# The first load of a soft-MoE kernel: one transfer of 128 rows, or four of 32 rows with a step of four partitions

## Chip, cores and metric

The kernel runs on one core of a Trainium2 chip. The metric is the device time in microseconds, the median over runs. Three runs of the kernel before took 174.36, 174.44 and 174.56 us. One more execution was profiled; its trace gives the rows below.

## What is computed

Linear attention over 8 batches of 8 heads, followed by a soft mixture of 8 experts with 4 slots each:

```python
# q, k, v: (8, 8, 576, 64)
kv  = einsum('bhsd,bhse->bhde', k, v)
out = einsum('bhsd,bhde->bhse', q, kv)
out = out / sqrt(mean(out*out, -1) + 1e-6) * g_norm
x   = out as (4608, 512)                     # tokens x (heads*dim)
logits = x @ phi                             # phi: (512, 32)
d = softmax of logits over the tokens
slot_input = d.T @ x                         # (32, 512), 4 slots for each expert
slot_out[e] = relu(slot_input[e] @ w1[e]) @ w2[e]   # w1: 512 x 1024, w2: 1024 x 512
c = softmax of logits over the slots
return c @ slot_out                          # (4608, 512)
```

All data is float32.

## The kernel before

The inputs are laid out on the host so that each load is one transfer of 128 rows, one row for each partition of SBUF. Nearly everything lands in one tile, `arena`, whose places are used again as data is done with. All loads and stores are issued by SP, in the order of the program, on one queue.

The first load, `first_in`, is 128 rows of 2448 floats: the router weights phi and g_norm (the first 144 columns), and the first half of k and v of batch 0. Behind it SP issues the second half of batch 0 (`kv_in`), half of q of the first pair of batches (`q0_in`), the two halves of kv of batch 1, the rest of `q0_in`, kv of batch 2 and part of `q1_in`. Line numbers: the first load is L123, and the others go through `load_row` (L85). The later ones wait until PE is done with the place that they fill.

PE begins with matmuls on constants (L457 and L467, `fill`), which need no load. Then, for each batch, it forms the 64 x 64 products of k and v from the loaded rows, contracting over 128 partitions (`Kv.products`, L195, and the border rows, L210), transposes them and multiplies them with phi (L224, L226). ACT and DVE copy the result into the block-diagonal tiles `bd`, and PE multiplies q with these, token tile by token tile (`products`, L263). DVE scales phi by g_norm once (`gphi`, L158), out of the first load. The statistics of the softmax over the tokens are kept as the tiles go by. After the last tile come the experts (`expert_h`, L638, and `expert_y`, L656, with the weights loaded by `load_w`, L114) and the outputs (L701, stored at L718).

The completion of a load is signalled by one of eight semaphores, `DMAHW0` to `DMAHW7`, which the framework hands out in turn, in the order of the issues. The ninth load takes the first one's semaphore again, and its issue waits until that earlier load has landed.

Of the kernel before, what the change touches and what calls it, by code (L numbers as in the profile page):

```python
# [55 lines left out]
HEAD = 144  # L56
# [10 lines left out]
def soft_moe_linear_attention(ctx: ExitStack, tc: tile.TileContext, first_in, kv_in, q0_in, q1_in, kv4_in, kv5_in, t3_in, w_in, out):  # L67


    nc = tc.nc  # L70
# [3 lines left out]
    arena = const.tile([P, HEAD + ARENA], F32, name="arena")  # L74
# [9 lines left out]
    def load_row(at, src):  # L84
        nc.sync.dma_start(place(at, src.shape[-1]), src)  # L85
# [34 lines left out]
        return parts[k][:, at : at + 256]  # L120


    nc.sync.dma_start(arena[:, : HEAD + 2304], first_in)  # L123
    load_row(KV_AT[0] + 9, kv_in[0, :, 2304:])
    load_row(Q_AT[0], q0_in[:, :2048])
    load_row(KV_AT[1], kv_in[1, :, :2304])
# [297 lines left out]
    first = {b: 9 * (b // 2) + 4 * (b % 2) for b in range(B)}  # L424
# [341 lines left out]
def build_program():  # L766
    import concourse.bacc as bacc

    nc = bacc.Bacc("TRN2", target_bir_lowering=False, num_devices=1, dynamic_dma_scratch_size=SCRATCH)
    shapes = {  # L770
        "first": (P, HEAD + 2304), "kv": (4, P, TOK), "q0": (P, TOK), "q1": (P, 2048),
        "kv4": (P, 2560 + TOK), "kv5": (P, 2 * TOK), "t3": (P, 3 * TOK),
        "w": (1, 2 * NE * P * UNIT),
    }
    args = [nc.dram_tensor(f"in_{n}_dram", s, F32, kind="ExternalInput").ap() for n, s in shapes.items()]
    args.append(nc.dram_tensor("out_0_dram", (1, 4 * NCH * P * 4 * CT * NS), F32, kind="ExternalOutput").ap())
    with tile.TileContext(nc, schedule_with_timeline_sim=True) as tc, tc.manual_schedule():
        soft_moe_linear_attention(tc, *args)
    return nc
# [58 lines left out]
```

## Time and profile before

| what | value |
|---|---|
| median of 3 runs | 174.44 us (174.36 to 174.56) |
| span of the profiled execution | 172.9 us |
| PE busy | 150.1 us (87%) |
| DVE, ACT, POOL busy | 86.3, 89.0, 57.2 us |
| moved by DMA | 71.67 MB, mean 414 GB/s |
| busy share of the 16 DMA engines, the program's own queue | 97.0% |
| mean granted clock of TensorE | 0.976 |

The span runs from the first to the last instruction of the profiled execution. The profile gives no other time for that execution; the median of the runs, which take in what lies around the span, is 1.5 us longer. "Idle" in a row of an engine is the time just before the instruction in which the engine did nothing, and behind the arrow stands what ended it. Windows of DMA count a packet, with all its bytes, where it starts.

### The profile page before, as it was taken

To read this page: it belongs to the slowest core of one execution; us is meant where nothing else is said; L and a number is where in the kernel's file an instruction comes from. 1 tells how busy PE (TensorE), PEld (TensorE's weight loads), DVE (VectorE), ACT (ScalarE), POOL (GpSimd) and SP (SyncE) were. 2 spreads that over 40 slices of the span, in tenths; PEclk is the share of its full clock that TensorE was granted. 3 is DMA by queue.
4 is the path that set the end of the run, shared out by engine and by line. 5 is a ranking of instruction groups with operands and counts; after the bars stand their busy time and mean duration, and the time that the engine had idled before them with its cause. 6 is when DMAs were issued, how large, how long until landed. Compare 5 with 4: busy or idle time off the path is not lost.

```text
span 172.9 us, 4638 instructions
## 1 busy us (share of the span) xinstructions
PE 150.1 (87%) x1975; PEld 109.0 (63%) x1975; DVE 86.3 (50%) x184; ACT 89.0 (51%) x230; POOL 57.2 (33%) x68
## 2 busy tenths in 40 slices
PE   7888897989999899999899989889999989989300
PEld 3457777889688888898796766346665544545000
DVE  1122156383677364763926897625887036228300
ACT  2036486787966888668759863203223035227400
POOL 6000708548356665456582489100000000000000
PEclk9999999999999999999999999999999999999955
DMA  5999999999999998999999998999999999999994
GB/s 188 417 429 426 446 403 449 438 424 471 413 409 443 479 461 359 394 453 402 451 468 428 426 425 368 426 445 400 459 419 428 425 425 403 443 392 401 453 392 199
DMA packets 3476, 71.67 MB, mean 414 GB/s; under 512 B 384, under 2 KB 384, under 8 KB 384
## 3 DMA queue, kind: packets, MB, share of 16 engines
q1 hardware_dynamic: 3456, 71.38, 97.0%
q8 instruction: 15, 0.25, 0.6%
q14 instruction: 5, 0.04, 0.1%
HBM read 61.94 MB, written 9.44 MB: 413 GB/s over the span
## 4 chain that ended last, share of the span: by engine, by line
PE 50%; DMA 23%; ACT 10%; DVE 6%; issue 3%; SPq 2%; DVEq 0%
PE o L263 16%; DMA arena<-in_kv_dram 13%; DMA arena<-in_w_dram 10%; PE kvp_kv L195 8%; PE po L701 5%; PE pY L656 5%; PE pS L412 4%; PE ph L638 2%; PE fill L467 2%; ACT sq L273 2%; PE o L254 2%; ACT arena L712 2%; ACT bd L230 1%; ACT xall L281 1%; SPq L85 1%
## 5 line engine op out<-in xcount | busy, mean ns | idle before, releaser
L263 PE MATMUL o<-bd,arena 128*128 128x192 f32 x256 | 49.3, 336 | 1.7 <-ACT bd L240 1.1
L263 PEld LDWEIGHTS o<-bd,arena 128*128 128x128 f32 x256 | 40.8, 190 | 5.0 <-ACT bd L240 1.6
L286 DVE TENSOR_REDUCE ms<-sq 128x16 f32<-128x1024 f32 (+1 forms) x19 | 22.1, 1162 | 32.2 <-ACT sq L273 32.0
L313 POOL TENSOR_TENSOR xall<-xall,r 128x512 f32<-128x512 f32 x34 | 34.8, 1046 | 0.0
L335 POOL TENSOR_TENSOR part<-part,r 128x512 f32<-128x512 f32 x17 | 17.8, 1050 | 50.4 <-DVE r L304 44.9
L273 ACT ACTIVATE sq<-o 128x512 f32<-128x512 f32 x36 | 21.5, 598 | 11.9 <-PE o L263 11.6
L281 ACT COPY xall<-o 128x512 f32<-128x512 f32 x34 | 20.6, 606 | 0.0
L195 PE MATMUL kvp_kv<-arena 128*64 128x64 f32 x480 | 17.3, 225 | 2.6 <-DMA arena<-in_kv_dram 1.9
L195 PEld LDWEIGHTS kvp_kv<-arena 128*64 128x64 f32 x480 | 15.2, 138 | 6.5 <-DMA arena<-in_kv_dram 2.8
L348 DVE TENSOR_REDUCE logits<-part 128x64 f32<-128x512 f32 (+1 forms) x18 | 17.8, 992 | 0.0
L656 PE MATMUL pY<-arena,xall 128*32 128x256 f32 x256 | 15.0, 380 | 0.2 <-DMA arena<-in_w_dram 0.2
L701 PE MATMUL po<-logits,z 32*128 32x384 f32 x96 | 12.8, 521 | 1.5 <-ACT arena L712 0.9
L638 PE MATMUL ph<-arena,sTe 128*32 128x256 f32 x224 | 12.7, 379 | 0.3 <-DVE sTe L585 0.3
L712 ACT COPY arena<-po 128x768 f32<-128x768 f32 x12 | 9.1, 801 | 7.4 <-PE po L701 7.4
L714 DVE COPY arena<-po 128x768 f32<-128x768 f32 x10 | 9.3, 955 | 7.0 <-PE po L701 7.0
L656 PEld LDWEIGHTS pY<-arena,xall 128*32 128x32 f32 x256 | 8.4, 110 | 6.7 <-issue 1.6
L280 ACT COPY part<-o 128x256 f32<-128x256 f32 x34 | 12.6, 370 | 0.0
L412 PE MATMUL pS<-xall,d 128*32 128x129 f32 x288 | 10.8, 277 | 1.2 <-ACT d L400 1.1
L701 PEld LDWEIGHTS po<-logits,z 32*128 32x128 f32 x96 | 6.1, 183 | 7.1 <-ACT arena L712 4.2
L638 PEld LDWEIGHTS ph<-arena,sTe 128*32 128x32 f32 x224 | 7.2, 110 | 5.3 <-DVE sTe L585 0.7
L412 PEld LDWEIGHTS pS<-xall,d 128*32 128x32 f32 x288 | 7.2, 109 | 4.4 <-issue 3.5
L294 ACT ACTIVATE r<-ms,eps 128x16 f32<-128x16 f32 x17 | 5.2, 308 | 5.9 <-DVE ms L286 5.9
(99 smaller groups left out, 148.3 us busy)
## 6 DMA issues: line engine op xcount, KB each, us to landing
arena<-in_w_dram SPq DMA_DIRECT2D x4, 4096.0 KB, 19.8
arena<-in_w_dram SPq DMA_DIRECT2D x1, 7168.0 KB, 27.6
arena<-in_t_dram SPq DMA_DIRECT2D x1, 6912.0 KB, 36.4
arena<-in_w_dram SPq DMA_DIRECT2D x1, 5120.0 KB, 17.8
arena<-in_kv_dram SPq DMA_DIRECT2D x2, 2304.0 KB, 23.6
arena<-in_kv_dram SPq DMA_DIRECT2D x1, 4608.0 KB, 43.1
out_dram<-arena SPq DMA_DIRECT2D x2, 2304.0 KB, 9.5
arena<-in_kv_dram SPq DMA_DIRECT2D x1, 3584.0 KB, 32.3
```

The costliest lines, as they stand in the source:

```text
L195: nc.tensor.matmul(self.pkv[lo : lo + 64, w, g], lhsT=main[:, w, 1, c, lo : lo + 64], rhs=main[:, w, 0, c, lo : lo + 64], start=c == 0 and ...
L263: nc.tensor.matmul(o[:, r, :192], lhsT=q_main(2 * g + i)[:, r, at : at + P], rhs=bds[i][:, r], start=True, stop=True)
L273: nc.scalar.activation(sqs[s][:, T - starts[s]], o[:, :, 32:160], AF.Square, scale=0.125)
L281: nc.scalar.copy(xts[T % NX][:, :, :128], o[:, :, 32:160])
L286: nc.vector.tensor_reduce(out=mss[s], in_=sqs.pop(s).rearrange("p t j (w d) -> p (t j w) d", w=2), axis=AX.X, op=ALU.add)
L313: nc.gpsimd.tensor_tensor(out=x, in0=x, in1=r[:, i].rearrange("p (j w) -> p j w", w=2).unsqueeze(3).to_broadcast([P, 4, 2, D]), op=ALU.mult,)
L335: engine.tensor_tensor(out=part, in0=part, in1=rs_of[s].unsqueeze(3).to_broadcast([P, STAGES[s], H, NS]), op=ALU.mult)
L348: nc.vector.tensor_reduce(out=L[:, pos(starts[s]) : pos(starts[s]) + STAGES[s]], in_=parts.pop(s).rearrange("p t h n -> p t n h"), axis=AX ...
L412: nc.tensor.matmul(pS[32 * j : 32 * j + 32], lhsT=ds[G][:, i], rhs=x[:, j], start=i == 0, stop=i == GROUPS[G] - 1)
L638: nc.tensor.matmul(ph[32 * j : 32 * j + 32], lhsT=sTe[:, (4 * e + c) * NS : (4 * e + c + 1) * NS], rhs=w_block("w1", e, 4 * c + j), start= ...
L656: nc.tensor.matmul(pY[32 * j : 32 * j + 32, hf, :256], lhsT=hTs[e][:, c], rhs=w_block("w2", u, at + c), start=e == 0 and c < 4, stop=e == ...
L701: nc.tensor.matmul(po[:, 0 if apart else u, : CT * NS].rearrange("p (g x) -> p g x", g=2), lhsT=z[f][lo : lo + 32], rhs=cT[k][lo : lo + 32 ...
```

## The change

The first load is issued as four transfers. Transfer i fills the partitions i, i+4, i+8 and so on up to i+124 (32 rows with a step of four partitions). On the host the rows of `first_in` are put in this order, so that each transfer reads 32 rows that lie together in memory.

```diff
-    nc.sync.dma_start(arena[:, : HEAD + 2304], first_in)
+    for i in range(4):
+        nc.sync.dma_start(arena[i::4, : HEAD + 2304], first_in[32 * i : 32 * i + 32])
     load_row(KV_AT[0] + 9, kv_in[0, :, 2304:])
     load_row(Q_AT[0], q0_in[:, :2048])
...
-        "in_first_dram": first,
+        "in_first_dram": np.concatenate([first[i::4] for i in range(4)]),
```

SP's queue from its first issue on, before. The names are those of the tensors; what stands in brackets is what the issue waits for (`DMAHW0_49` is the semaphore DMAHW0, `PE_49` PE's):

```order
L123 DMA arena<-in_first_dram 128x2448
L85 DMA arena<-in_kv_dram 128x2304
L85 DMA arena<-in_q_dram 128x2048
L85 DMA arena<-in_kv_dram 128x2304 x2
L85 DMA arena<-in_q_dram 128x2560
L85 DMA arena<-in_kv_dram 128x4608
L85 DMA arena<-in_q_dram 128x2048
L85 DMA arena<-in_kv_dram 128x4608 [waits DMAHW1_49,DMAHW0_49,PE_49]
```

The same place now:

```order
L124 DMA arena<-in_first_dram 32x2448 x4
L85 DMA arena<-in_kv_dram 128x2304
L85 DMA arena<-in_q_dram 128x2048
L85 DMA arena<-in_kv_dram 128x2304 x2
L85 DMA arena<-in_q_dram 128x2560 [waits DMAHW0_49]
L85 DMA arena<-in_kv_dram 128x4608 [waits DMAHW1_49]
L85 DMA arena<-in_q_dram 128x2048 [waits DMAHW2_49]
L85 DMA arena<-in_kv_dram 128x4608 [waits DMAHW4_49,DMAHW3_49,PE_49]
```

The four transfers take the semaphores 0 to 3, the next four loads 4 to 7, and the sixth, seventh and eighth load of before take 0 to 2 again and wait for them. Every load has moved down by three places.

PE's queue at its first use of a load, before, between the last `fill` and the products of batch 0:

```order
L467 MATMUL fill<-ones 128x512
L195 MATMUL kvp_kv<-arena 64x64 [waits DMAHW0_49]
L195 MATMUL kvp_kv<-arena 64x64 x15
L210 MATMUL kvp_kv<-arena 64x64 x4
L457 LDWEIGHTS zeros
```

And now:

```order
L468 MATMUL fill<-ones 128x512
L196 MATMUL kvp_kv<-arena 64x64 [waits DMAHW2_49,DMAHW3_49,DMAHW1_49,DMAHW0_49]
L196 MATMUL kvp_kv<-arena 64x64 x15
L211 MATMUL kvp_kv<-arena 64x64 x4
L458 LDWEIGHTS zeros
```

The order is the same; the first product waits for all four transfers. So does DVE's first use of phi.

## Rows read from the trace of the kernel before

**Rows 1.** Page, the span in 40 slices, busy share of the DMA engines in tenths.

```profile
DMA  5999999999999998999999998999999999999994
```

**Rows 2.** Page: DMA packets, and the queues with packets, MB, share of 16 engines' span.

```profile
DMA packets 3476, 71.67 MB, mean 414 GB/s; under 512 B 384, under 2 KB 384, under 8 KB 384
...
q1 hardware_dynamic: 3456, 71.38, 97.0%
q8 instruction: 15, 0.25, 0.6%
```

**Rows 3.** Chain that ended last, in order of time: start, length, what.

```profile
3.81 23.08 DMA arena<-in_kv_dram
...
118.15 17.48 DMA arena<-in_w_dram
```

**Rows 4.** Timeline of PE: start, length, line, operation, count, idle time before.

```profile
6.35 1.15 PE L195 MATMUL kvp_kv<-arena 128*64 128x64 f32 x32 [0.72 <-DMA arena<-in_first_dram]
...
9.18 1.15 PE L195 MATMUL kvp_o<-arena 128*64 128x64 f32 x32 [0.25 <-DMA arena<-in_kv_dram]
...
26.93 1.15 PE L195 MATMUL kvp_kv<-arena 128*64 128x64 f32 x32 [1.16 <-DMA arena<-in_kv_dram]
...
135.77 3.66 PE L656 MATMUL pY<-arena,xall 128*32 128x256 f32 x64 [0.23 <-DMA arena<-in_w_dram]
```

**Rows 5.** Windows 4 to 12 and 16 to 26 us: engines, clock, DMA share, GB/s.

```profile
4.00:12.00 8.00, 6.78 (x95) 4.30 (x94) 1.01 (x4) 1.40 (x6) 0.00 (x0) 1.00 1.00 422
...
16.00:26.00 10.00, 9.12 (x118) 7.65 (x114) 4.02 (x9) 6.64 (x19) 3.05 (x3) 1.00 1.00 426
```

**Rows 6.** DMA issues: transfer, count, KB each, median us from issue to landing.

```profile
arena<-in_kv_dram SPq DMA_DIRECT2D x2, 2304.0 KB, 23.6
...
arena<-in_kv_dram SPq DMA_DIRECT2D x3, 1152.0 KB, 13.4
...
arena<-in_q_dram SPq DMA_DIRECT2D x2, 1024.0 KB, 17.5
...
arena<-in_q_dram SPq DMA_DIRECT2D x1, 1280.0 KB, 18.1
arena<-in_first_dram SPq DMA_DIRECT2D x1, 1224.0 KB, 5.6
```

**Rows 7.** Windows of the first 4 us: the last two columns are DMA share, GB/s.

```profile
1.00:2.00 1.00, 0.95 (x3) 0.40 (x4) 0.37 (x1) 1.00 (x1) 0.70 (x4) 1.00 0.49 69
2.00:3.00 1.00, 1.00 (x4) 0.45 (x3) 0.00 (x0) 0.01 (x1) 1.00 (x4) 1.00 0.58 186
3.00:4.00 1.00, 1.00 (x2) 0.41 (x2) 0.00 (x0) 0.00 (x0) 0.81 (x2) 1.00 1.00 421
...
1.60:1.80 0.20, 0.20 (x2) 0.01 (x1) 0.11 (x1) 0.20 (x1) 0.03 (x1) 1.00 1.78 245
...
2.20:2.40 0.20, 0.20 (x2) 0.09 (x1) 0.00 (x0) 0.00 (x0) 0.20 (x2) 1.00 1.42 343
```

**Rows 8.** Timeline of SP's issues: start, length, line, transfer, count.

```profile
0.74 0.38 SPq L123 DMA_DIRECT2D arena<-in_first_dram  x1
1.17 0.42 SPq L85 DMA_DIRECT2D arena<-in_kv_dram  x1
...
3.28 0.49 SPq L85 DMA_DIRECT2D arena<-in_q_dram  x1
...
4.30 0.47 SPq L85 DMA_DIRECT2D arena<-in_q_dram  x1
10.67 1.28 SPq L85 DMA_DIRECT2D arena<-in_kv_dram  x3
```

**Rows 9.** Instructions of line 85, SP's wait steps: ns min/median/max, first and last start.

```profile
L85 SPq EVENT_SEMAPHORE  x3: 28/28/28, 9.1 to 26.9; - x3
```

**Rows 10.** The last store's issue, and the window in which its rows start.

```profile
162.28 0.33 SPq L718 DMA_DIRECT2D out_dram<-arena  x1
...
163.00:163.20 0.20, 0.00 (x0) 0.00 (x0) 0.00 (x0) 0.00 (x0) 0.00 (x0) 1.00 3.02 1290
```

## Prediction

> **What bounds the kernel now.** I read the slices of the span first. The DMA row stands at 8 or 9 from the second slice to the last but one, so the 16 DMA engines are never out of work between the start and the last store [rows 1]. The queue table says the same as one number: the program's own queue keeps the 16 engines busy for 97.0% of the span [rows 2]. Then I read the chain that ended last. It starts with the issues on SP, runs 23.08 us along one load of kv (batch 2, 2304 KB), which lands just before 26.93, goes through PE and ACT without another load until 118.15, waits 17.48 us for a load of weights, and ends in the output copies and the store issued at 162.28 [rows 3, 10]. PE's own rows agree: it idles for loads at 6.35 (0.72 us), at 9.18 (0.25) and longest at 26.93 (1.16), and next only at 135.77 (0.23) [rows 4].
>
> So the first 27 us belong to the loads, and all that follows hangs on the time at which kv of batch 2 lands. That time is the start of the stream plus the bytes ahead of it at a fixed rate. The rate is 422 to 426 GB/s in every stretch from 4 to 26 us [rows 5]. The loads up to kv of batch 2 hold 1224+1152+1024+1152+1152+1280+2304 = 9288 KB [rows 6], or 9.51 MB, or 22.4 us at 425 GB/s.
>
> The start is what the change touches. A window counts a row where it starts. By 4.00 us the engines have started 69+186+421 = 676 KB, which is 1.59 us of the full rate, so the stream runs as if it had begun at 4.00-1.59 = 2.41 us [rows 7]. The first rows start between 1.6 and 1.8 us (245 GB/s over 0.2 us is 49 KB, five rows of 9.8 KB), some 0.9 us after SP begins the issue at 0.74 [rows 7, 8]; seven more start only between 2.2 and 2.4 (343 GB/s). Were all engines at their rate from 1.7, the stream would be 0.71 us earlier. That is all there is to gain.
>
> By the rate alone kv of batch 2 would land at 2.41+22.4 = 24.8; it lands at 26.89, 2.1 us later, because a load is complete only when the slowest engine has its rows. One source of such lag is in the queue table: 15 instruction fetches take 0.6% of 16 engines' span, 16.6 us in all, 1.1 us each, and each falls on one engine [rows 2]. A better start of the other engines therefore need not reach the landing in full.
>
> **The change part by part.** The bytes, their rows and their places stay the same.
>
> *Four issues for one.* On SP eight issues began between 0.74 and 4.30, 0.51 us apart on average, the second 0.43 us after the first [rows 8]. So the quarters go out at about 0.74, 1.25, 1.76 and 2.27, and the second load at 2.78 instead of 1.17. With 0.86 to 1.06 us from issue to first rows, the fourth quarter is ready at 3.1 to 3.3. The stream needs its rows after three quarters of 2.95 us (1.25 MB at 425 GB/s), at 2.41+2.21 = 4.62. Cover 1.3 us, cost nothing. The second load is ready at 3.6 to 3.8 and needed at 5.36. Cover 1.5 us, cost nothing.
>
> *New waits on SP.* The program has eight completion semaphores for loads. The four quarters use four of them, so the issues of q0's second half, kv of batch 2 and q1 now wait for the first, second and third quarter to land, where they waited for nothing. At worst they leave at 6.34, when the whole first load lands today (0.74 + 5.6), instead of 3.28 to 4.30 [rows 6, 8], and the last of them at about 7.8. Ahead of them the queue then holds 1152+1024+1152+1152 = 4480 KB, 4.59 MB, 10.8 us, which lasts until 2.41+2.95+10.8 = 16.2 us. Cost nothing; if that cover were gone, 3 us. Behind them on SP stands the load of kv for batch 3, which waits for PE anyway and went out at 10.67 [rows 8]. All later loads wait for the same transfers as before.
>
> *PE's and VectorE's first wait.* They wait for four semaphores instead of one. The only rows of such a wait step are SP's, 28 ns each [rows 9]; three more are 0.08 us. PE has this back at 9.18 and at 26.93, where it idles. Cost nothing to 0.08, taken as nothing.
>
> *More packets.* The trace has 384 packets under 512 B for 24 transfers, 16 each [rows 2], so 48 more, three on each engine. The first two loads end in the stretch from 4 to 12 us (PE starts on them at 6.35 and 9.18), which runs at 422 GB/s against 426 from 16 to 26 [rows 4, 5]; even if that 1% were all theirs, it is 0.08 us for two ends, 0.12 for three. Between 0 and 0.12; I take 0.05.
>
> *The start of the stream.* A quarter has two rows for each engine instead of eight. If the late starts (seven rows at 2.2 to 2.4) come from dealing out 128 rows, a quarter's 32 are dealt in a fourth of the time and up to 0.71 us is gained. If they come from cold engines or memory, nothing is. The nearest row is the last store: also 128 rows, issued at 162.28 to engines of which most had run dry. There 1290 GB/s over 0.2 us, 258 KB or ten rows of 24.6 KB, start together between 163.0 and 163.2, the same 0.7 to 0.9 us after the issue [rows 10]. So 128 rows are dealt to idle engines within 0.2 us, and the spread at the start is more likely a cold start, which the quarters share. I take 0.2 us of gain, nearer to nothing than to 0.71.
>
> Sum on the profile's execution: 172.9 - 0.2 + 0.05 = 172.75 us of span. The median of the runs, 174.44, lies 1.5 us above that span; I leave this as it is. **174.3 us**, 0.1% less, which a measurement of this kernel can't tell from no change (I take 0.2%, 0.35 us, as that limit).
>
> [...]
>
> **The rivals.**
>
> *All engines start with the first ones.* The gain is 0.4 to 0.71 us, time 173.7 to 174.0. For it: the first rows are spread over 0.8 us, in two bursts [rows 7]. Against it: the store's ten rows in 0.2 us, and the one lagging engine on which the landing hangs.
>
> *Engines collide on the way into SBUF.* In a transfer of 128 rows each engine holds 26.6 GB/s, a sixteenth of 425. If the stepped rows are dealt so that two engines write into the same part of SBUF at one time, each of the pair has half of that: the first load takes up to 5.9 us instead of 2.95, and everything behind moves by 1.5 (half the rows collide) to 2.95 us: 175.9 to 177.4. It decides as soon as some 12% of the rows collide (0.35 us of 2.95). Nothing here shows a stepped transfer, which is for it; against it, rows four partitions apart cover all of the 128 partitions as evenly as before. [...]
>
> *The quarters run one after the other.* If a quarter's rows wait until the last has landed, each pays again what lies around the data: 5.6 us from issue to landing less 2.95 of data is 2.65 us, three times 8 us, 182.4; if each pays only the 0.9 us to its first rows, 2.7 us, 177.1. For it: the first quarter meets an empty queue. Against it: the queued loads pay nothing of the kind. [...]
>
> **How the numbers follow.** The forecast (174.1 to 174.75, the start as it is or a little better) has 0.50, all engines early 0.31, collisions 0.13, quarters in a row 0.06. All early is faster by over 0.2%, the two last are slower: 0.31, 0.50, 0.19. The range 173.7 to 175.0 holds the first two cases, 0.81; its upper end leaves room for a collision of a few rows.
>
> **What would show it.** After the change the stretch from 1 to 4 us should start about 676 KB again, up to 85 KB more for my 0.2 us; over 850 KB would be the first rival; under 500 KB a collision or quarters in a row. PE should start L196 between 5.7 and 6.5, and batch 2's products at 26.7 to 27.0. SP should show three short waits for the first load and issue kv of batch 3 at about 10.7 again. I am wrong if the first load's rate falls, or if kv of batch 2 moves while the start doesn't: then an instruction fetch has fallen on another engine.

## The result

The changed kernel takes 175.82 us (median of 4 runs, 175.48 to 176.03), the one before beside it 174.47 (174.36 to 174.56): a ratio of 1.0077, with an interval of 1.0064 to 1.0089. The forecast was 174.3, no change that can be measured. The kernel is slower by 1.35 us and lies outside the range of 173.7 to 175.0. The profiled execution has a span of 174.2 us against 172.9, and the same granted clock, 0.976.

The windows of the first 10 us after the change; the last two columns are the DMA share and GB/s, with each row of the transfers counted where it starts:

```profile
1.00:2.00 1.00, 0.95 (x3) 0.41 (x4) 0.37 (x1) 1.00 (x1) 0.71 (x5) 1.00 0.00 0
2.00:3.00 1.00, 1.00 (x4) 0.45 (x3) 0.00 (x0) 0.01 (x1) 1.00 (x4) 1.00 0.97 245
3.00:4.00 1.00, 1.00 (x2) 0.40 (x2) 0.00 (x0) 0.00 (x0) 0.80 (x2) 1.00 1.04 402
4.00:5.00 1.00, 1.00 (x3) 0.47 (x2) 0.00 (x0) 0.00 (x0) 0.00 (x0) 1.00 0.87 255
5.00:6.00 1.00, 1.00 (x3) 0.20 (x1) 0.00 (x0) 0.00 (x0) 0.00 (x0) 1.00 0.95 387
...
0.00:10.00 10.00, 7.59 (x54) 3.67 (x54) 1.10 (x4) 1.68 (x3) 2.92 (x13) 1.00 0.78 293
```

And the same windows of the kernel before, from 4 us on:

```profile
4.00:5.00 1.00, 1.00 (x3) 0.53 (x2) 0.00 (x0) 0.00 (x0) 0.00 (x0) 1.00 0.96 401
5.00:6.00 1.00, 0.63 (x2) 0.00 (x0) 0.00 (x0) 0.00 (x0) 0.00 (x0) 1.00 1.06 434
...
0.00:10.00 10.00, 7.92 (x82) 4.34 (x84) 1.55 (x6) 2.07 (x4) 2.93 (x13) 1.00 0.81 319
```

No row starts before 2.0 us, where before 69 KB had [rows 7]. Then the engines start almost together, and by 4.00 us they have started 647 KB against 676: so far 0.07 us are lost. The loss comes after that. Between 4 and 6 us the engines start 642 KB instead of 835, which is 0.45 us of the full rate; by 10 us it is 2930 against 3190 KB, 0.61 us. In the slow window rows are not only missing, those that start there also take longer: 255 KB for 0.87 of the engines' time against 401 KB for 0.96, that is 1.4 times as long for a byte. That is how rows look at the start of a stream (245 KB for 0.97 between 2 and 3 us).

The chain that ended last, after the change:

```profile
0.73 0.54 SPq L124
...
1.32 0.57 SPq L124
...
1.94 0.59 SPq L124
...
2.57 0.59 SPq L124
...
3.21 0.58 SPq L85
...
5.90 21.59 DMA arena<-in_kv_dram
...
27.54 1.15 PE kvp_kv L196 x32
...
35.16 36.97 DMA arena<-in_t_dram
```

The issue of a quarter takes SP 0.54 to 0.59 us instead of 0.38, so the four go out 0.62 us apart and the second load at 3.21 instead of 1.17 [rows 8]. The chain again runs along kv of batch 2, but it now goes on along a second load, `in_t_dram` (6912 KB, issued once PE is through with an earlier place).

PE's waits for loads, after:

```profile
7.40 1.15 PE L196 MATMUL kvp_kv<-arena 128*64 128x64 f32 x32 [1.28 <-DMA arena<-in_first_dram]
...
27.54 1.15 PE L196 MATMUL kvp_kv<-arena 128*64 128x64 f32 x32 [1.18 <-DMA arena<-in_kv_dram]
...
72.26 1.28 PE L196 MATMUL kvp_kv<-arena 128*64 128x64 f32 x32 [0.59 <-DMA arena<-in_t_dram]
```

The wait at 72.26 is new. In the trace before, the same products start without a wait for a load:

```profile
71.13 1.15 PE L195 MATMUL kvp_kv<-arena 128*64 128x64 f32 x32
```

The DMA view after the change, with its packets and two of its issues (count, KB each, median us to landing):

```profile
DMA packets 3524, 71.67 MB, mean 411 GB/s; under 512 B 432, under 2 KB 432, under 8 KB 432
...
arena<-in_t_dram SPq DMA_DIRECT2D x1, 6912.0 KB, 37.0
...
arena<-in_first_dram SPq DMA_DIRECT2D x4, 306.0 KB, 3.8
```

So the span's 1.3 us are made up thus: PE starts on batch 2 0.61 us later (27.54 against 26.93, [rows 4]); at the load `in_t_dram` 0.52 us are added (72.26 against 71.13 is 1.13 in all); the remaining 0.2 come after that. (Against the second trace of the kernel before, e12 below, the same two places and the span are 0.69, 1.38 and 1.6 us later: a share is good to some 0.3 us.) The load `in_t_dram` was issued at 34.55 before and landed 36.4 us later, at 70.95, only 0.18 us ahead of its use. After the change it is issued 0.61 us later, as PE is, and takes 37.0.

### The profile page after: what moved, and what is told of

Same layout as the page of the kernel before. It is cut to its first block, busy times and chain, and to the rows that moved or that the text cites. A ratio compares the mean times of both kernels' runs of the same rounds, so it can differ in the third digit from the quotient of the medians.

```text
span 174.2 us, 4645 instructions
## 1 busy us (share of the span) xinstructions
PE 151.0 (87%) x1975; PEld 110.8 (64%) x1975; DVE 86.3 (50%) x184; ACT 89.1 (51%) x230; POOL 57.1 (33%) x68
## 2 busy tenths in 40 slices
DMA packets 3524, 71.67 MB, mean 411 GB/s; under 512 B 432, under 2 KB 432, under 8 KB 432
## 4 chain that ended last, share of the span: by engine, by line
PE 39%; DMA 34%; ACT 7%; DVE 6%; issue 3%; SPq 3%; POOL 1%; POOLq 1%; DVEq 0%
DMA arena<-in_t_dram 21%; DMA arena<-in_kv_dram 12%; PE pY L657 9%; PE ph L639 8%; PE o L264 8%; PE po L702 5%; PE kvp_kv L196 4%; ACT arena L713 2%; SPq L85 1%; ACT sq L274 1%; DVE ms L287 1%; SPq L124 1%; PE fill L468 1%; DVE logits L349 1%; ACT xall L282 1%
## 5 line engine op out<-in xcount | busy, mean ns | idle before, releaser
L196 PE MATMUL kvp_kv<-arena 128*64 128x64 f32 x480 | 17.4, 225 | 3.3 <-DMA arena<-in_kv_dram 1.4
L196 PEld LDWEIGHTS kvp_kv<-arena 128*64 128x64 f32 x480 | 15.4, 138 | 7.2 <-issue 4.1
L657 PE MATMUL pY<-arena,xall 128*32 128x256 f32 x256 | 15.8, 380 | 0.0
L657 PEld LDWEIGHTS pY<-arena,xall 128*32 128x32 f32 x256 | 9.6, 110 | 5.9 <-issue 1.7
L468 PE MATMUL fill<-ones 128*128 128x512 f32 x16 | 8.6, 678 | 0.0
```

The costliest lines, as they stand in the source:

```text
L196: nc.tensor.matmul(self.pkv[lo : lo + 64, w, g], lhsT=main[:, w, 1, c, lo : lo + 64], rhs=main[:, w, 0, c, lo : lo + 64], start=c == 0 and ...
L657: nc.tensor.matmul(pY[32 * j : 32 * j + 32, hf, :256], lhsT=hTs[e][:, c], rhs=w_block("w2", u, at + c), start=e == 0 and c < 4, stop=e == ...
```

## The experiments

The theories, by the letters of the expectations: a quarter gives each engine only two rows and, in the stepped form, is handed over slowly, so that the engines run dry between quarters (A); the change makes the engines write into the same part of SBUF (B); the new order of the rows in memory is slow to read (C); or, from e5 on, it is the split itself, at a queue that is still empty (D). All kernels compute the whole result. Each time is a median, and each ratio is taken against runs of the kernel before beside it (medians 174.42 to 174.48).

**e1: neighbouring partitions.** Four quarters of 32 neighbouring partitions, memory as before.

```diff
-    nc.sync.dma_start(arena[:, : HEAD + 2304], first_in)
+    for i in range(4):
+        nc.sync.dma_start(arena[32 * i : 32 * i + 32, : HEAD + 2304], first_in[32 * i : 32 * i + 32])
```

> Four quarters of 32 neighbouring partitions (no step), host layout as before. Theory A (a quarter gives each engine only two rows at an empty queue; the engines run dry between quarters): about as the changed kernel, 175.5 to 176.0, rows of 0.37 us once running, some 380 GB/s or less from 4 to 6 us. Theory B (the stepped destination makes engines collide in SBUF): without the step the collisions are gone, 174.5. Theory C (32 rows that lie together in memory are read slowly): as the changed kernel. If instead neighbouring partitions are what collides, the first load runs at half rate, some 210 GB/s, 3 us later: 177 or more.

Measured: 177.17 us, ratio 1.0154 (1.0139 to 1.0169). Its windows:

```profile
3.00:4.00 1.00, 1.00 (x2) 0.41 (x2) 0.00 (x0) 0.00 (x0) 0.80 (x2) 1.00 1.05 215
4.00:5.00 1.00, 1.00 (x3) 0.53 (x2) 0.00 (x0) 0.00 (x0) 0.00 (x0) 1.00 0.91 206
5.00:6.00 1.00, 0.69 (x2) 0.00 (x0) 0.05 (x1) 0.00 (x0) 0.00 (x0) 1.00 1.07 235
...
7.00:8.00 1.00, 0.00 (x0) 0.00 (x0) 0.00 (x0) 0.00 (x0) 0.00 (x0) 0.94 0.94 195
```

The engines are as busy as ever and move half: 195 to 235 GB/s, until the first load is in. (PE idles 3.03 us for it and then has a granted clock of 0.50, which adds to the time.) Half the rate at full busy time is what the prediction had worked out for engines that collide on the way into SBUF, and the step of four partitions avoids it: the changed kernel reaches 402 GB/s between 3 and 4 us. The windows show the rate alone; that it comes from a collision is the prediction's reading.

**e2: the memory order.** Stepped on both sides, the host's layout as before.

```diff
-    nc.sync.dma_start(arena[:, : HEAD + 2304], first_in)
+    for i in range(4):
+        nc.sync.dma_start(arena[i::4, : HEAD + 2304], first_in[i::4])
```

> Stepped on both sides: each quarter reads every fourth row of the host layout of before, so its 32 rows no longer lie together in memory. Theory A: no change against the changed kernel, 175.8 within 0.4, and again a stretch of less than 300 GB/s near 4 to 5 us. Theory C: the slow stretch is gone, kv of batch 2 lands at 27.0 or before, time 174.5 to 174.8. Theory B: as the changed kernel.

Measured: 175.81 us, ratio 1.0089 (1.0059 to 1.0119), as the change. Its windows, and two of PE's waits:

```profile
3.00:4.00 1.00, 1.00 (x2) 0.41 (x2) 0.00 (x0) 0.00 (x0) 0.80 (x2) 1.00 0.99 392
4.00:5.00 1.00, 1.00 (x3) 0.53 (x2) 0.00 (x0) 0.00 (x0) 0.00 (x0) 1.00 0.98 245
```

```profile
27.13 1.15 PE L196 MATMUL kvp_kv<-arena 128*64 128x64 f32 x32 [1.18 <-DMA arena<-in_kv_dram]
...
71.97 1.29 PE L196 MATMUL kvp_kv<-arena 128*64 128x64 f32 x32 [0.72 <-DMA arena<-in_t_dram]
```

The slow window is there without the new order in memory, so C falls. With 0.98 of busy time counted to that window and only 245 KB moved, most of the loss there is rows that are slow, not rows that are missing. PE starts on batch 2 at 27.13 and then waits 0.72 us for `in_t_dram`, until 71.97. Again the loss comes in two places, but with the same bytes by 10 us (294 against 293 GB/s) only 0.20 us of it shows at batch 2, where the change loses 0.61.

**e3: two queues.** The quarters alternate between SP's queue and ACT's.

```diff
-        nc.sync.dma_start(arena[i::4, : HEAD + 2304], first_in[32 * i : 32 * i + 32])
+        (nc.sync, nc.scalar)[i % 2].dma_start(arena[i::4, : HEAD + 2304], first_in[32 * i : 32 * i + 32])
```

> The stepped quarters issued in turn by SP and by ACT, so that all four are handed over by about 2 us instead of 3.2. Theory A (late hand-over and dry engines): the stretch from 4 to 6 us is full, over 400 GB/s, and kv of batch 2 lands at 26.9 or earlier, time 174.2 to 174.8. Theories B and C: the rows are as slow as before, 402+255+387 KB between 3 and 6 us as in the changed kernel, time 175.5 to 176.

Measured: 174.97 us, ratio 1.0035 (1.0025 to 1.0044). Its windows:

```profile
4.00:5.00 1.00, 1.00 (x3) 0.47 (x2) 0.00 (x0) 0.00 (x0) 0.00 (x0) 1.00 0.91 372
5.00:6.00 1.00, 1.00 (x3) 0.20 (x1) 0.00 (x0) 0.00 (x0) 0.00 (x0) 1.00 1.11 445
```

The slow stretch is nearly gone, PE starts on batch 2 at 26.97, and there is no wait for `in_t_dram`. So with the stepped quarters handed over by 2.2 us instead of 3.2, 0.85 us of the 1.35 come back; A's expectation (over 400 GB/s in both windows, 174.2 to 174.8) is just missed. It remains 0.5 us slower than before, and no run shows where. The saved issue time may be all of the 0.85 us or a part; e6, which also issues sooner, gains only 0.35, but differs in its rows, and no run tells the saved time from the second queue itself.

**e4: the second load split instead.** The first load whole, the second as four stepped quarters.

```diff
-    load_row(KV_AT[0] + 9, kv_in[0, :, 2304:])
+    for i in range(4):
+        nc.sync.dma_start(place(KV_AT[0] + 9, 2304)[i::4], kv_in[0, i::4, 2304:])
```

> The first load is one transfer as before, and the second load (second half of batch 0) goes out as four stepped quarters with stepped source. The engines then have the first load to work on while the quarters are handed over. Theory A: no cost, full rate from 3 to 10 us, 174.4 to 174.6. Theory B: the second load is slow by as much as the first was, 175.0 to 175.8. Theory C: no statement, the source is stepped too.

Measured: 174.69 us, ratio 1.0015 (1.0005 to 1.0024). Its windows:

```profile
4.00:5.00 1.00, 1.00 (x3) 0.47 (x2) 0.00 (x0) 0.00 (x0) 0.00 (x0) 1.00 1.00 421
5.00:6.00 1.00, 1.00 (x3) 0.20 (x1) 0.00 (x0) 0.00 (x0) 0.00 (x0) 1.00 1.00 414
```

The same split, with the same slow issues, costs the stream nothing once a whole load is queued ahead of it: 322 GB/s over the first 10 us, batch 2 at 26.88. In the time some 0.2 us remain, which no row explains.

**e5: two halves.** Two transfers of 64 rows with a step of two.

```diff
-    nc.sync.dma_start(arena[:, : HEAD + 2304], first_in)
+    for i in range(2):
+        nc.sync.dma_start(arena[i::2, : HEAD + 2304], first_in[64 * i : 64 * i + 64])
...
-        "in_first_dram": first,
+        "in_first_dram": np.concatenate([first[i::2] for i in range(2)]),
```

> Two stepped transfers of 64 rows (step of two partitions) instead of four of 32: four rows for each engine and transfer, 1.47 us of work against some 0.6 us for an issue. Theory A (stepped quarters are handed over too slowly for two rows of work each): first rows again at about 2.0 us, but no stretch under 350 GB/s before 6 us, kv of batch 2 at 27.0 to 27.2, time 174.6 to 175.1. Theory D (each transfer at an empty queue pays a restart): half of the loss of four, about 175.1, with a slow stretch where the second one begins.

Measured: 175.35 us, ratio 1.0052 (1.0037 to 1.0067). Its windows:

```profile
2.00:3.00 1.00, 1.00 (x4) 0.45 (x3) 0.00 (x0) 0.01 (x1) 1.00 (x4) 1.00 1.05 284
3.00:4.00 1.00, 1.00 (x2) 0.41 (x2) 0.00 (x0) 0.00 (x0) 0.80 (x2) 1.00 0.95 382
4.00:5.00 1.00, 1.00 (x3) 0.47 (x2) 0.00 (x0) 0.00 (x0) 0.00 (x0) 1.00 1.02 411
5.00:6.00 1.00, 1.00 (x3) 0.20 (x1) 0.00 (x0) 0.00 (x0) 0.00 (x0) 1.00 1.05 351
6.00:7.00 1.00, 0.23 (x1) 0.00 (x0) 0.00 (x0) 0.00 (x0) 0.00 (x0) 1.00 0.90 342
```

The slow stretch has moved from 4 to 5 us to 5 to 7 us, so it doesn't go with a fixed time. Nor does it stand where D expected it, at the start of the second half: that half begins at 627 KB, just before 4 us (284 + 382 = 666 KB by then), and 411 GB/s follow. The slow stretch begins near 5.5 us, where the two halves, 1253 KB, are through and the second load follows. In the change and in e2, 647 and 666 KB have started by 4 us, so there it begins behind two quarters, also 627 KB. In all three it thus begins as the third transfer of the queue is taken up; why, no run shows. PE starts on batch 2 at 27.14 and waits 0.54 us for `in_t_dram`, until 71.81. The time, 175.35, lies above both expectations (up to 175.1).

**e6: columns.** Four transfers of all 128 rows and 612 columns each; no step, no new order.

```diff
+    for i in range(4):
+        nc.sync.dma_start(arena[:, 612 * i : 612 * i + 612], first_in[:, 612 * i : 612 * i + 612])
```

> Four transfers again, but of 128 rows without a step and a quarter of the columns each (2.4 KB rows, eight for each engine). The bytes of a transfer and the waits on semaphores are those of the changed kernel; the form of the issue is that of before (0.38 to 0.43 us). Theory A: first rows at 1.75 us, full rate from 3 us on, time 174.4 to 174.6. Theory D (four transfers at an empty queue, whatever their form): slow from 4 to 6 us as in the changed kernel, 175.3 or more.

Measured: 175.47 us, ratio 1.0063 (1.0046 to 1.0080). Its windows, and then SP's first issues:

```profile
3.00:4.00 1.00, 1.00 (x2) 0.41 (x2) 0.23 (x1) 0.00 (x0) 0.81 (x2) 1.00 1.06 389
4.00:5.00 1.00, 1.00 (x3) 0.47 (x2) 0.34 (x2) 0.00 (x0) 0.00 (x0) 1.00 0.96 318
5.00:6.00 1.00, 1.00 (x5) 0.24 (x5) 0.00 (x0) 0.00 (x0) 0.00 (x0) 1.00 1.06 341
```

```profile
0.74 1.81 SPq L124 DMA_DIRECT2D arena<-in_first_dram  x4
2.58 0.43 SPq L85 DMA_DIRECT2D arena<-in_kv_dram  x1
```

The issues are plain ones, 0.46 us apart, and the second load leaves 0.63 us earlier than after the change; the stretch from 4 to 6 us is slow nevertheless, and PE starts on batch 2 at 27.72. So the slow stretch doesn't need the stepped form and its slower issues (A falls), and of the theories D is left. The comparison isn't clean, though: the rows of 2.4 KB also move less for the same busy time, before the slow stretch already (389 KB for 1.06 of the engines' time between 3 and 4 us, against 421 for 1.00 [rows 7]), and no run says how much of this loss is theirs. Here PE starts on the products at `in_t_dram` at 71.68 without a wait.

**e7: the first load from ACT's queue.** The load of before, whole, issued by ACT.

```diff
-    nc.sync.dma_start(arena[:, : HEAD + 2304], first_in)
+    nc.scalar.dma_start(arena[:, : HEAD + 2304], first_in)
```

> The kernel before with its one first load issued by ACT instead of SP. It prices the use of a second queue by itself, for the run with two queues, whose loads landed as before but which took 0.5 us more. If the second queue costs something outside the loads: 174.8 to 175.0 with loads that land as before. If not: 174.3 to 174.5.

Measured: 175.69 us (174.93 to 176.60 over 10 runs), ratio 1.0075 (1.0051 to 1.0100). It didn't measure what it was made for. The first load shares the engines with SP's loads and lands late, as PE's row shows:

```profile
9.45 1.98 PE L195 MATMUL kvp_kv<-arena 128*64 128x64 f32 x32 [3.36 <-DMA arena<-in_first_dram]
```

After 3.36 us without work the 32 products take 1.98 us instead of 1.15, at a granted clock of 0.50. The time is lost at PE, not in the stream (314 GB/s over the first 10 us).

**e8, e9: a pure delay.** One or two loads of 128 rows by 16 floats into a tile of their own, which nothing uses, ahead of the whole first load.

```diff
+    ahead = const.tile([P, 16], F32, name="ahead")
+    nc.sync.dma_start(ahead, first_in[:, :16])
     nc.sync.dma_start(arena[:, : HEAD + 2304], first_in)
```

> The kernel before with one more small load (128 rows of 64 bytes, not used) issued ahead of the first load, which so leaves 0.43 to 0.47 us later. It shows what a later start of the stream by itself costs. If the time follows the start one to one: 174.8 to 175.0, kv of batch 2 at 27.3 to 27.4. If a late start is made worse behind (as 0.6 us at kv of batch 2 became 1.3 in the changed kernel): 175.2 or more. If the slow first rows are a cold start that the small load takes on itself: 174.3 to 174.6.

> Two small loads ahead of the first load instead of one, so that it leaves about 0.9 us later than in the kernel before. One cost 1.0 us for 0.45 us of delay. If the time follows the start of the stream one to one with a fixed share on top: kv of batch 2 at 27.9 to 28.1 and 175.7 to 176.0. If each step costs 1.0: 176.4. If the extra was chance: 175.3 to 175.5.

Measured: e8 175.44 us, ratio 1.0056 (1.0039 to 1.0072); e9 175.72, ratio 1.0069 (1.0052 to 1.0086). The windows of e8:

```profile
2.00:3.00 1.00, 1.00 (x4) 0.45 (x3) 0.00 (x0) 0.01 (x1) 1.00 (x4) 1.00 0.76 148
3.00:4.00 1.00, 1.00 (x3) 0.42 (x3) 0.00 (x0) 0.00 (x0) 0.81 (x2) 1.00 0.91 362
```

and of e9:

```profile
2.00:3.00 1.00, 1.00 (x4) 0.45 (x3) 0.00 (x0) 0.01 (x1) 1.00 (x4) 1.00 0.71 97
3.00:4.00 1.00, 1.00 (x2) 0.41 (x2) 0.00 (x0) 0.00 (x0) 0.81 (x2) 1.00 0.61 215
4.00:5.00 1.00, 1.00 (x3) 0.47 (x2) 0.00 (x0) 0.00 (x0) 0.00 (x0) 1.00 0.97 401
```

If the slow start were cold engines or cold memory that a first small load warms, the large load would start at its full rate. It starts in the same slow way, only later. The first load is issued 0.43 us later in e8 (1.17) and 0.90 later in e9 (1.64); PE starts on batch 2 at 27.58 and 27.92, 0.65 and 1.0 us later; the time is 1.0 and 1.3 us longer. So a delay at the start is paid for, but not in proportion: the first 0.43 us cost 1.0 us, the next 0.47 only 0.3.

**e10, e11: a backlog ahead of the quarters.** e11 issues the second load first and then the first, both whole; e10 does the same with the first load in the change's four quarters.

```diff
-    nc.sync.dma_start(arena[:, : HEAD + 2304], first_in)
     load_row(KV_AT[0] + 9, kv_in[0, :, 2304:])
+    for i in range(4):
+        nc.sync.dma_start(arena[i::4, : HEAD + 2304], first_in[32 * i : 32 * i + 32])
...
-        "in_first_dram": first,
+        "in_first_dram": np.concatenate([first[i::4] for i in range(4)]),
```

> The four stepped quarters as in the changed kernel, but the second load (128 rows, 1152 KB) is issued ahead of them, so that the engines have 2.8 us of work when the first quarter is handed over. Theory A or D (the loss is made where quarters meet empty engines): full rate, over 400 GB/s, in every microsecond from 3 to 10, first rows at 1.75, and the same time as the kernel with this order and one transfer, within 0.3 us. Theory E (quarters of 32 rows are slow wherever they stand): a stretch under 350 GB/s between 4 and 8 us, and 0.5 us or more over that kernel.

> The kernel before with the second load issued ahead of the first, both as one transfer: what the order by itself costs, beside the run with quarters in that order. The first products wait some 2.7 us longer, kv of batch 2 lands as before. If PE keeps its clock and the time hangs on kv of batch 2: 174.4 to 174.7. If PE loses its clock in the longer wait: up to 176.

Measured: e10 176.52 us, ratio 1.0120 (1.0093 to 1.0146); e11 175.35 (174.71 to 177.11 over 10 runs), ratio 1.0058 (1.0034 to 1.0083). The windows of e10:

```profile
4.00:5.00 1.00, 1.00 (x3) 0.47 (x2) 0.00 (x0) 0.00 (x0) 0.00 (x0) 1.00 0.96 406
5.00:6.00 1.00, 1.00 (x3) 0.20 (x1) 0.00 (x0) 0.00 (x0) 0.00 (x0) 1.00 1.07 451
```

and the first of e11, for the start of a stream:

```profile
1.00:2.00 1.00, 0.95 (x3) 0.40 (x4) 0.37 (x1) 1.00 (x1) 0.70 (x5) 1.00 0.98 138
```

The change's own quarters run at the full rate when a whole load is ahead of them (316 GB/s over the first 10 us, e11 317), so they are not slow wherever they stand (E falls), and they don't collide with one another (B falls). Their total times say nothing of the stream: in both PE waits some 3 us for the first load, and its clock is at 0.50 for a while afterwards. A and D expected e10 within 0.3 us of e11. Why it is 1.2 us above although their streams are alike is not settled; both spread by more than 1 us from run to run.

**e12: the kernel before once more**, as a measure of how far two traces of one kernel differ.

> The kernel before once more, for a second trace of it: how far kv of batch 2 (PE at 26.93), the end of the weights (135.77) and the span (172.9) differ between two executions. By the runs' own spans, 172.5 to 172.9, all three within 0.3 us, and the start (69+186+421 KB by 4 us) within 20 KB.

Measured: 174.50 us, ratio 1.0005 (0.9994 to 1.0015), span 172.6 against 172.9. PE starts on batch 2 at 26.85 (26.93), and the first 10 us move 323 GB/s (319). Differences below 0.1 us at that place, or below 4 GB/s there, are not read above; further on the two traces differ more, by 0.25 us at `in_t_dram` (70.88 against 71.13). None of the versions tried beats the kernel before; e4 comes nearest.

## Why the prediction was wrong

*What held.* The kernel hangs on the start of the stream and on kv of batch 2: PE still waits there, 1.18 us against 1.16. The stepped quarters don't collide (402 GB/s between 3 and 4 us, against the 195 to 235 of e1). The price worked out for the collision rival, 175.9 to 177.4, is where e1 came out with neighbouring rows (177.17, some of it from PE's lower clock); that the change itself, at 175.82, lies next to that price is chance. SP's new waits cost nothing: it issued the loads back to back up to 6.41 us, and kv of batch 3 at 11.81, about 1.1 us later, as PE is. The 48 packets are there (3524 against 3476). The list of PE's waits for loads left out two, at 15.54 us (0.54) and at 18.34 (0.16); nothing in the sum hangs on them. The lag of a load's last completion is in the trace before: of the 16 completions of kv of batch 2, 15 come between 25.05 and 25.69 us and one at 26.89. This lag is there from the first load that lands after the first instruction fetch (one packet at 13.28, 0.94 us long); in the three loads before it all 16 lie within 0.65 to 0.71 us.

*"Four issues for one ... Cover 1.3 us, cost nothing" failed.* The step worked with 0.51 us from issue to issue and with a stream that moves a queued quarter at its fixed rate. SP needed 0.62 us, and the first quarter's rows began more than 1.2 us after its issue instead of 0.9. More important, the engines didn't move the quarters at that rate, although the fourth was issued at 2.57, more than 1.4 us ahead of the slow stretch at 4: between 4 and 5 us they were busy for 0.87 of the time and took 1.4 times as long for a byte. The two microseconds from 4 to 6 cost the stream 0.45 us, where the step had nothing. The evidence that queued loads follow one another at 422 GB/s [rows 5] came from a stretch with several loads queued. The start of the stream is another state: the same split costs the stream nothing behind a backlog (322 GB/s over the first 10 us in e4, where the kernel before has 319, and 316 in e10, where e11 has 317), and costs 0.9 to 1.4 us of the time at an empty queue in every form tried on one queue that reaches all partitions (the change, e2, e5, e6).

*"The spread at the start is more likely a cold start" failed.* e8 and e9 contradict it, as far as one or two small loads can warm anything. Its row, the last store, showed ten rows that start together, not 128. The other reading, dealing out the rows, isn't borne out either: in e11 128 rows go first too, and 138 KB start between 1 and 2 us, against 69 before and 98 in e12. With the quarters the engines start nearly together, 245 KB between 2 and 3 us against 186, but the first rows come later. By 4 us 0.07 us are lost where 0.2 of gain was put.

*"The sum"* carried the shift at kv of batch 2 to the end unchanged. That shift was 0.61 us; the time moved by 1.35. That the stream, too, is 0.61 us behind by 10 us is in part chance: e2 and e5 are as far behind by then (294 and 295 GB/s) and start on batch 2 only 0.20 and 0.21 us later, so the bytes moved don't by themselves set when that load is complete. The prediction called the stretch up to 118 us free of loads, because no wait stood there. It had not looked how near the next load was to becoming one: `in_t_dram` had landed 0.18 us before its use. The 1.5 us that the sum put between span and median came from two different executions; within one it is 1.8 (176.03 and 174.2 after, 174.41 and 172.6 in e12), so the forecast was 0.3 us low for that alone.

*The stated signs.* The test of the bytes was too short: up to 4 us it found 647 KB where about 676 were due, and would have passed, while the loss lies in the two microseconds after that. The other signs showed it: PE started L196 at 7.40 (5.7 to 6.5 were stated) and batch 2 at 27.54 (26.7 to 27.0), SP issued kv of batch 3 at 11.81 (10.7), and the first load's rate fell, which the prediction had named as the way to be wrong.

*Which rival.* The quarters in a row was the nearest in kind: the split costs something at an empty queue, but 0.6 us of stream in all, not 2.7 to 8, and not by a price for each transfer (the second half of e5 begins at full rate). It had 0.06 of the chance; the state of the queue, which was the argument for it, should have weighed more.

*Open.* Why the engines falter between 4 and 6 us is not settled. Shown is what it isn't: the order in memory (e2), collisions in SBUF or the place of the data (the same quarters run at the full rate in e10, 406 and 451 GB/s between 4 and 6 us); that it doesn't need the stepped form (e6); and that two queues heal most of it (e3). Engines that run dry (A) may have a share in the change, where their busy time fell to 0.87; in e2 it was 0.98 and the window as slow. And why `in_t_dram` takes 37.0 us instead of 36.4 is only argued: from 27 to 72 us the engines together move as much as before (19.5 MB by the windows), so perhaps one engine is further behind than the rest, and the uneven start put it there; no row here shows single engines. It happened in the change, e2 and e5, and not in e6, e8 and e9, which lost their time otherwise.

## What to carry to other kernels

Leave the first load of a saturated stream whole: here splitting it saved nothing in any form, and cost its extra issues and a second faltering stretch (0.5 us of the time in e3, 0.9 to 1.4 in e5, e6, e2 and the change), while the same split behind a queued load was free at the stream (322 GB/s over the first 10 us in e4 against 319). When a load ahead of everything moves, look up for every later load how long before its use it lands, not only which ones are waited for today. If a transfer must cover 32 partitions, step through all 128 instead of taking neighbours (402 against 195 to 235 GB/s here), though not on the first load.

## What the runs showed of the hardware

- Transfers to 32 neighbouring partitions, one after the other on one queue, ran at 195 to 235 GB/s in e1; with a step of four partitions they reached 402 after the change.
- SP took 0.54 to 0.59 us to issue a transfer with a step of four partitions after the change, and 0.38 for the plain one of 128 rows at the same place before.
- In e7, PE's idle time of 3.36 us was followed by half the clock (0.50 of full speed) for several microseconds; after the change its idle time of 1.28 us at the same place left the clock at 1.00. The windows of e7 from 8 us on show how long:

```profile
8.00:10.00 2.00, 0.55 (x10) 0.56 (x12) 0.47 (x2) 0.00 (x0) 0.00 (x0) 0.67 1.01 425
10.00:12.00 2.00, 2.00 (x37) 1.64 (x33) 0.10 (x1) 0.09 (x1) 0.00 (x0) 0.50 1.01 426
12.00:14.00 2.00, 2.00 (x15) 1.15 (x16) 0.15 (x1) 0.70 (x3) 0.00 (x0) 0.50 1.01 429
14.00:16.00 2.00, 2.00 (x37) 1.61 (x33) 0.29 (x2) 0.10 (x1) 0.00 (x0) 0.62 1.02 433
```

The same was seen at waits of 2.96 (e10), 3.03 (e1) and 3.20 us (e11): the 32 products behind them took 1.93 to 1.98 us instead of 1.15.
